# A second Strassen-Winograd level in the down projection of a two-layer block on one Trainium2 core

## Chip, core and metric

The kernel runs on one core of a Trainium2 chip. A core has five engines with an instruction queue each: TensorE (PE, the matrix multiplier; PEld is its loading of the stationary operand), VectorE (DVE), ScalarE (ACT), GpSimd (POOL) and SyncE (SP, which here issues all DMA transfers, in order). SBUF is the on-chip memory of 128 partitions, PSUM the accumulators that TensorE writes: eight banks of 128 x 512 float32 here. The metric is the device time of one execution in microseconds, as the median of several runs.

## The reference

Two blocks, A (linear attention) and B (a bilinear gated feed-forward), are applied in the order A, B, A, B with residual connections and a layer norm ahead of each. There are 2048 tokens, a width D of 1024 and a hidden width F of 3584.

```
def _B_ref(x, w_gate, w_up, w_down):
    g = x @ w_gate            # 2048x1024 @ 1024x3584
    u = x @ w_up
    return (g * u) @ w_down   # 2048x3584 @ 3584x1024

x = x + _A_ref(_layernorm(x), wqkv, wo)
x = x + _B_ref(_layernorm(x), w_gate, w_up, w_down)
x = x + _A_ref(_layernorm(x), wqkv, wo)
x = x + _B_ref(_layernorm(x), w_gate, w_up, w_down)
```

Block A projects q, k and v, applies a positive feature map to q and k, and works with sums over the tokens instead of an attention matrix. The change does not touch its arithmetic.

## The kernel before, in words

`_Prog` collects operations for each engine with the SBUF bytes and PSUM banks that they read and write, and derives the semaphore waits. Each engine's order is the order in which the code adds its operations, so the code below is a schedule written out by hand.

Block B (`layer_B`) works in two passes of 1024 tokens in each layer: four passes in all, called pass 1 to 4 here (`first` and `ps_` number them: (True, 0), (True, 1), (False, 0), (False, 1)). A pass has two stages.

`gateup` computes h = g * u. Products are taken with the Strassen-Winograd scheme, seven half-size products in place of eight: a matrix product in 2 x 2 blocks, C = A B, becomes M1 = A11 B11, M2 = A12 B21, M3 = S4 B22, M4 = A22 T4, M5 = S1 T1, M6 = S2 T2, M7 = S3 T3, where S and T are sums and differences of blocks of A and B. In passes 2 to 4 products 2 and 4 of this stage are split once more in the same way (`L2SETS`, "24"), with matmuls of 256 columns at L1044 beside those of 512 at L951. A pass has 14 pairs of weight units; the strings in `ORDERS` write out the order of each pair's steps: P, D and digits are matmul groups, F evicts a result into h and R issues two weight loads. A mark ' on a step means that it runs one pair later, so the last pair's are left over for `tail()`. The results lie in four blocks of h, hA to hD, each [128, 14, 512] in float16.

`down` multiplies h by w_down. It runs the seven products of the first level in the order 1 2 7 4 6 5 3 (`DPROD`). Each product has four blocks of 128 tokens (t = 0 to 3), and each block is 14 matmuls (two half groups of seven) into one PSUM bank: 7 x 4 x 14 = 392 matmuls of 128 x 128 by 128 x 512 in a pass, at L1199. Products alternate between the bank sets `B_DX` and `B_DV`. After a block, VectorE evicts the bank with `stt` (L624: times a scale, plus a partial sum or the residual), and makes a difference of two h blocks for a later product with `tt` (L621, 14 x 128 elements). The first product's first half group is added ahead of `tail()`.

The weights come through a ring of five SBUF slots of 8 KB a partition. `ring_issue` (DMA issues appear at L393) loads the next item into the slot that is freed next: in `gateup` a unit of gate or up weights, with its sums from DRAM; in `down` half of a product's weights (896 KB), two items a product. The w_down blocks for products 1, 2 and 3 are read from the input; the sums T for 5, 6, 7 and 4 are made once in pass 1 and kept in DRAM (`t_scratch`). The callbacks `dticks0` and `dticks1` (called for each block of a product) store x to DRAM (`stash`), run the sums that the next pass needs (`tq`, made of `t_ops` and `tp_ops`), load the weights of the next block A (`load_w`) and advance its layer norm (`nxt`).

Of the kernel before, what the change touches and what calls it, by code (L numbers as in the profile page):

```python
# [180 lines left out]
def build_kernel(nc, A_x, A_wqkv, A_wo, B_w_gate, B_w_up, B_w_down, out):  # L181
# [16 lines left out]
        "": "P1A P1B D2A F1A D2B F1B R P6A P6B T0 P7A P7B D4A F4A D4B F4B P5A F2A P5B F2B D3A F3A D3B F3B T1",  # L198
        "24": "F4A' P1A F4B' P1B 21 F3A' F3B' 25 P6A 26 T1' T0 P6B 27 D2A F1A P7A 41 P7B D2B P5A F1B P5B F2A F2B 45 46 D3A R 47 D3B D4A D4B S24+",
    }  # L200
    MUL_ENG = "pool"
    SZ_W = KT * D * 2
# [60 lines left out]
    P = _Prog(V_D + NJ * 32)  # L263
# [17 lines left out]
    KOUT = dkey("out")  # L281
    KTA = [dkey("ta%d" % i) for i in range(2)]
# [8 lines left out]
    tscr = nc.dram_tensor("t_scratch", (4, 128, NJ, 512), F16, kind="Internal").ap()  # L291
    nscr = nc.dram_tensor("xn_scratch", (S, D), F16, kind="Internal").ap()

    from contextlib import ExitStack
    with ExitStack() as es:
# [68 lines left out]
        B_DX = [7, 4, 5, 6]  # L364
        B_DV = [0, 2, 1, 3]
# [8 lines left out]
        def R(o, n):  # L374
            return [(o, o + n)]
# [204 lines left out]
        def ring_begin(first):  # L580
            RG.update(n=0, first=first, tq=None)

# [5 lines left out]
        NPASS = NU + 14  # L588
        DPROD = ["1", "2", "7", "4", "6", "5", "3"]
# [3 lines left out]

        def ring_issue():
            n = RG["n"]
            if n >= 2 * NPASS:
                return
            RG["n"] = n + 1
            o = r_slot(n)[0][0]
            ps_, u = divmod(n, NPASS)  # L600
            sl = (n + 1) % NR
            if u < NU:
# [3 lines left out]
                if not (RG["first"] and ps_ == 0):  # L606
                    dma(vh(o + 4096, 2048), sscr[u], r_slot(n, 4096, 8192), KRS[sl], rd=R(V_S + u * 32, 32))
                return
            q, hf = divmod(u - NU, 2)
            q = DPROD[q]  # L610
            js = slice(hf * 7, hf * 7 + 7)
            if q in "123":
                e, d = {"1": (0, 0), "2": (1, 0), "3": (1, 1)}[q]
                dma(vb(o, 7 * 512).rearrange("p (j c) -> p j c", c=512), wd_v[:, js, e, d * 512:(d + 1) * 512], r_slot(n, 0, 7168), KRR[sl])
            else:
                t = {"5": 0, "6": 1, "7": 2, "4": 3}[q]
                dma(vh(o, 7 * 512).rearrange("p (j c) -> p j c", c=512), tscr[t][:, js, :], r_slot(n, 0, 7168), KRR[sl],
                    rd=R(V_D + hf * 7 * 32, 7 * 32))
# [55 lines left out]
        def store_s(n):  # L674
            u = n % NPASS
# [19 lines left out]
        def layer_A(lnp, nxt, first):  # L695
# [43 lines left out]
            def lnstep(i, h):  # L739
# [638 lines left out]
```

## Time and profile before

| | us |
|---|---|
| median of three runs (1490.14 to 1492.62) | 1490.62 |
| the profiled execution's own time | 1492.19 |
| its span, first to last instruction | 1490.2 |
| PE busy | 1472.2 |
| DVE busy | 1065.6 |
| ACT busy | 479.8 |
| POOL busy | 439.0 |
| `down` of pass 1, from-to in the span | 415.4 to 500.0 |
| `down` of pass 2 | 666.7 to 752.3 |
| `down` of pass 3 | 1151.1 to 1236.7 |
| `down` of pass 4 | 1401.6 to 1487.4 |

A row of a group of instructions reads: line, engine, operation, output from input, shapes, count | busy us in all, mean ns of one | idle time of the engine just before them, and what ended it. `ps` is PSUM, `arena` is SBUF. Matmuls are pipelined: a matmul's duration in such a row is longer than the distance between the starts of two, and the distance is what a stream of them costs. A row in order of time has the start, the time to the end of the merged instructions, and in brackets the idle time before and its releaser. A row by windows has the time in the window, busy us of each engine with counts, the granted TensorE clock, the busy share of the DMA engines, and GB/s.

### The profile page before, as it was taken

The page shows a single profiled execution, that of the slowest core. Times are in us where ns is not written, and L with a number is a line of the kernel's source. Part 1 is how long each engine was busy: PE and PEld are TensorE (multiplying, and loading weights), DVE is VectorE, ACT ScalarE, POOL GpSimd, SP SyncE. Part 2 cuts the span into 40 slices and gives each one's busy share as a digit, 9 for nine tenths or more (in the row PEclk, how much of TensorE's full clock was granted, in tenths as well). Part 3 has the DMA queues.
Part 4 walks back from the last instruction along what each step waited for, and adds up shares of the span by engine and source line. Part 5 has one row for each costly group of instructions (what it writes and reads, how often), then busy time and mean ns, then how long its engine had stood idle before and what let it go on. Part 6 is the DMA issues. An engine that isn't in the chain of part 4 may idle for free.

```text
span 1490.2 us, 19805 instructions
## 1 busy us (share of the span) xinstructions
PE 1472.2 (99%) x7494; PEld 712.1 (48%) x7494; DVE 1065.6 (72%) x1862; ACT 479.8 (32%) x900; POOL 439.0 (29%) x435
## 2 busy tenths in 40 slices
PE   8999999999999999999999999999999999999999
PEld 4444444333344555554444444445555445555544
DVE  7986978778657588765488778787676565676653
ACT  3332356333300244440023314554444003444200
POOL 4544621212110144340044335314334002243300
PEclk9999999999999999999999999999999999999999
DMA  6134657698964667855465347656555655555542
GB/s 226 37 92 111 148 133 202 184 289 276 299 234 166 226 181 227 218 182 182 138 188 163 100 98 170 162 137 181 170 175 181 227 182 195 179 170 170 189 173 98
DMA packets 305263, 262.92 MB, mean 176 GB/s; under 512 B 102800, under 2 KB 266896, under 8 KB 305168
## 3 DMA queue, kind: packets, MB, share of 16 engines
q1 hardware_dynamic: 305168, 261.66, 58.4%
q8 instruction: 59, 0.97, 0.3%
q14 instruction: 36, 0.29, 0.1%
HBM read 199.23 MB, written 38.80 MB: 160 GB/s over the span
## 4 chain that ended last, share of the span: by engine, by line
PE 89%; DVE 4%; DMA 3%; issue 1%; POOL 1%; ACT 1%; SPq 0%; DVEq 0%; ACTq 0%
PE ps L951 32%; PE ps L1199 23%; PE ps L704 15%; PE ps L1044 9%; PE ps L786 7%; PE ps L872 2%; DMA arena<-arena 1%; DVE arena L621 1%; DVE arena L420 1%; DMA arena<-in_B_w_up_dram 1%; DMA arena<-in_A_wqkv_dram 1%; DMA arena<-in_B_w_gate_dram 1%; POOL arena L733 1%; PE ps L798 0%; PE ps L826 0%
## 5 line engine op out<-in xcount | busy, mean ns | idle before, releaser
L951 PE MATMUL ps<-arena 128*128 128x512 f16 x2464 | 588.6, 379 | 1.5 <-DMA arena<-in_B_w_up_dram 1.0
L624 DVE SCALAR_TENSOR_TENSOR arena<-ps,arena 128x512 f16<-128x512 f32 (+2 forms) x564 | 376.9, 687 | 239.7 <-PE ps L1199 151.2
L975 POOL TENSOR_TENSOR arena<-arena 128x512 f16<-128x512 f16 x196 | 222.9, 1164 | 453.4 <-DVE arena L624 453.3
L951 PEld LDWEIGHTS ps<-arena 128*128 128x128 f16 (+1 forms) x2464 | 232.7, 98 | 231.5 <-ACT arena L956 17.8
L1199 PE MATMUL ps<-arena 128*128 128x512 f16 (+1 forms) x1568 | 339.6, 379 | 2.4 <-DVE arena L624 2.4
L956 ACT ACTIVATE arena<-ps 128x512 f32<-128x512 f32 x308 | 183.9, 597 | 355.4 <-PE ps L951 349.9
L1199 PEld LDWEIGHTS ps<-arena 128*128 128x128 f16 x1568 | 153.2, 98 | 187.5 <-DVE arena L624 3.8
L621 DVE TENSOR_TENSOR arena<-arena 128x512 f16<-128x512 bf16 (+3 forms) x440 | 231.7, 564 | 11.4 <-DMA arena<-arena 3.6
L704 PE MATMUL ps<-arena 128*128 128x512 bf16 x1024 | 223.7, 379 | 2.8 <-ACT arena L524 1.1
L1044 PE MATMUL ps<-arena 128*128 128x256 f16 x1176 | 183.9, 273 | 3.4 <-DVE arena L621 2.2
L704 PEld LDWEIGHTS ps<-arena 128*128 128x128 f16 x1024 | 99.6, 98 | 121.7 <-DMA arena<-in_A_wqkv_dram 1.4
L1044 PEld LDWEIGHTS ps<-arena 128*128 128x128 f16 (+1 forms) x1176 | 111.0, 98 | 97.2 <-DVE ps L1051 26.7
L566 ACT ACTIVATE arena<-ps 128x512 f32<-128x512 f32 x128 | 76.4, 597 | 232.9 <-PE ps L704 218.4
L1051 DVE TENSOR_TENSOR ps<-ps,arena 128x256 f32<-128x256 f32 x168 | 72.3, 430 | 81.0 <-ACT ps L1048 76.3
L423 POOL TENSOR_SCALAR arena<-arena 128x1 f32<-128x1 f32 x64 | 20.7, 323 | 330.1 <-DVE arena L422 330.1
L786 PE MATMUL ps<-arena 128*128 128x512 bf16 x512 | 115.4, 379 | 0.0
L872 PE MATMUL ps<-arena 128*128 128x512 bf16 x512 | 111.4, 379 | 3.3 <-ACT ps L866 3.3
L733 POOL TENSOR_TENSOR arena<-arena 128x1024 f16<-128x1024 f32 x32 | 79.9, 2497 | 90.2 <-DVE arena L731 84.2
L716 POOL TENSOR_TENSOR arena<-arena 128x512 f32<-128x512 f32 x60 | 74.6, 1248 | 87.1 <-DVE arena L569 85.7
L420 DVE BATCH_NORM_STATS2 arena<-arena 128x6 f32<-128x512 bf16 x128 | 88.1, 688 | 13.1 <-DMA arena<-in_A_x_dram 6.1
L569 DVE SCALAR_TENSOR_TENSOR arena<-ps,arena 128x512 bf16<-128x512 f32 x128 | 88.5, 692 | 4.4
L567 DVE TENSOR_SCALAR arena<-arena 128x512 f32<-128x512 f32 x128 | 65.8, 514 | 27.9 <-ACT arena L566 26.6
(51 smaller groups left out, 612.9 us busy)
## 6 DMA issues: line engine op xcount, KB each, us to landing
arena<-s_scratch SPq DMA_DIRECT2D x84, 512.0 KB, 6.7
arena<-in_B_w_gate_dram SPq DMA_DIRECT2D x56, 512.0 KB, 6.1
arena<-in_B_w_up_dram SPq DMA_DIRECT2D x56, 512.0 KB, 6.2
arena<-t_scratch SPq DMA_DIRECT2D x32, 896.0 KB, 5.6
arena<-in_B_w_down_dram SPq DMA_DIRECT2D x24, 896.0 KB, 5.7
s_scratch<-arena SPq DMA_DIRECT2D x28, 512.0 KB, 6.5
arena<-in_A_wqkv_dram SPq DMA_DIRECT2D x12, 1024.0 KB, 8.1
x_scratch<-arena SPq DMA_DIRECT2D x32, 256.0 KB, 7.1
```

Source lines behind the costliest of these rows:

```text
L420: P.add("dve", (lambda h: lambda e: e.bn_stats(st[j][:, 6 * h:6 * h + 6], x_res[:, i, (D // 2) * h:(D // 2) * (h + 1)]))(h), rd=r_x(i, (D ...
L621: P.add("dve", lambda e: e.tensor_tensor(out=out, in0=a, in1=b, op=op), rd=rd, wr=wr, prd=prd)
L624: P.add("dve", lambda e: e.scalar_tensor_tensor(out=out, in0=a, scalar=sc, in1=b, op0=ALU.mult, op1=op1), rd=rd, wr=wr, prd=prd)
L704: return [e.matmul(psb(bank), xnT[:, k, i * 128:(i + 1) * 128], w[:, k, h * 512:(h + 1) * 512], start=(k == 0), stop=(k == KT - 1)) for k ...
L733: P.add("pool", lambda e: e.tensor_tensor(out=asb[b].rearrange("p (h c) -> p h c", c=32), in0=pbuf.rearrange("p (h c) -> p h c", c=32), in ...
L786: return [e.matmul(psb(bank), xr[:, t, j * 128:(j + 1) * 128], pk[:, h, t, :], start=(t == 0), stop=(t == NST - 1)) for t in range(NST)]
L872: return [e.matmul(psb(bank), xnT[:, g, i * 128:(i + 1) * 128], wp[:, g, dh * 512:(dh + 1) * 512], start=(dh == 0 and g == 0), stop=(g == ...
L951: P.add("pe", lambda e: [e.matmul(psb(bank), w[:, k, :], x[:, k, :], start=(start and k == 0), stop=(k == 3), skip_group_check=True) for k ...
L956: P.add("act", lambda e: e.activation(t, psb(bank), AF.Copy, scale=SG), prd=[bank], wr=r)
L975: P.add(MUL_ENG, lambda e: e.tensor_tensor(out=hx, in0=ut, in1=hx, op=ALU.mult), rd=ur + hr, wr=hr)
L1044: P.add("pe", lambda e: [e.matmul(psb(bank)[:, 256 * half:256 * half + 256], w[:, k, :], xx[:, k, :], start=(start and k == 0), stop=(k == ...
L1199: return [e.matmul(psb(bank), hv[:, 7 * hf + k, t * 128:(t + 1) * 128], w[:, k, :], start=(start and hf == 0 and k == 0), stop=(hf == 1 an ...
```

## The change

In passes 2, 3 and 4, products 1, 4, 5 and 3 of `down` are themselves computed by seven products of half the size in each dimension (`l2prod`). The token blocks are paired (t with t + 2, i = 0 and 1), the 14 parts of the contraction are split in two halves of seven, and the 512 output columns in two of 256. A second-level product is a sequence of seven groups, "1562734" (`DOPS`), each of 2 x 7 matmuls with 256 columns: 98 in place of 56 with 512. Groups 1, 6 and 7 accumulate in banks X, group 5 in Y, groups 2 and 3 in the two halves of A, group 4 in B. ScalarE copies X into A, B and two SBUF buffers (`acopy`), VectorE adds Y to a buffer into A and B (`dadd`), and then evicts A after group 3 and B after group 4.

The sums of h blocks (`l2sums`: four kinds for i = 0 and 1, of 7 x 128 elements each, for every second-level product) go to columns of the normalised, transposed x that the pass no longer needs. They stand in a list `bg`, together with the first level's 16 sums, and are taken from it in the numbers that the strings `POPS` give after each block or group (`pace`), or when a matmul group needs one (`need`). The first four sums of product 1 are issued in the last pair of `gateup`, at the new step H (`pre`). `POPS` also places the `tq` sums of the next pass.

The weight operands of the four products are kept ready in a new DRAM tensor, `d_images`, seven images of 7 x 256 columns each. They are made in pass 1: `make_images` takes four sums per product on VectorE out of the ring's slots, into 512-byte pieces in the same free columns, and stores them. For products 4 and 5 three raw quarters are stored from the ring as well, 22 stores in all; for 1 and 3 the raw quarters (six) are copied from DRAM to DRAM during the first block A (`raws`). In passes 2 to 4 such a product takes four ring items (two images each, the last one alone) instead of two.

The order of the products becomes 1 2 6 7 4 5 3, in pass 1 4 1 2 5 6 3 7; the bank sets become `B_DO` and `B_DS`; some PSUM accumulations and evictions move (product 7 now evicts to two destinations, and product 5 in passes 2 to 4). In pass 2 two empty ring items (`HOLES`) shift the slots. The q weights of the next block A are loaded after product 5, the k weights after group 5 of product 3, where both were loaded after product 5, k first. A second-level product calls its four ticks together at its end.

```diff
-        "24": "F4A' P1A F4B' ... D3A R 47 D3B D4A D4B S24+",
+        "24": "F4A' P1A F4B' ... D3A R 47 D3B H D4A D4B S24+",
+    DORDS = {(True, 0): "4125637", (True, 1): "1267453", (False, 0): "1267453", (False, 1): "1267453"}
+    DOPS = "1562734"
+    DL2 = {(False, 0): "", (False, 1): "1453", (True, 0): "1453", (True, 1): "1453"}
+    DIMG = "1453"
+    HOLES = {(True, 1, "6"), (True, 1, "7")}
+    PRE = "12"
+    POPS = {
+        (True, 0): "2222 2222 2222 2222 2222 2222 2222 / 0000 0000 0000 0000 1111 1111 0004",
+        (True, 1): "1111111 2222 2222 2222 2222211 2222211 2222211 /",
+        (False, 0): "1111111 2222 2222 2222 2222211 2222211 2222211 / 0 0000 1111 0000 0001111 1111111 1",
+        (False, 1): "1111111 2222 2222 2222 2222211 2222211 2222211 /",
+    }
...
-        B_DX = [7, 4, 5, 6]
-        B_DV = [0, 2, 1, 3]
+        B_DO = [4, 7, 2, 3]
+        B_DS = [0, 1, 5, 6]
...
+            elif kind == "l":
+                no = 1 if i == 3 else 2
+                qi = DIMG.index(u)
+                dma(vb(o, no * 1792), dimg[qi][:, 2 * i * 1792:(2 * i + no) * 1792], r_slot(n, 0, no * 3584), KRR[sl],
+                    rd=R(V_I + (qi * 7 + 2 * i) * 32, no * 32))
...
+                GOES = {"1": ["11"], "6": ["12"], "7": ["22", "21"] if own4 else ["22"], "4": ["21"], "2": ["11"], "5": ["22", "12"] if "3" in l2 else ["22"], "3": ["12"]}
...
+                def make_images(q, wsl):
...
+                    t1 = mk_(0, p12, p11, ALU.subtract)
+                    t3 = mk_(2, p22, p12, ALU.subtract)
+                    t2 = mk_(1, p22, st_[0], ALU.subtract)
+                    t4 = mk_(3, p21, st_[1], ALU.subtract)
+                    raws_ = [] if q in DWS else [lambda: put(*p11, "1"), lambda: put(*p22, "3"), lambda: put(*p21, "2")]
+                    return [raws_ + [t1], [t3, lambda: put(*st_[0], "5")], [t2, t4, lambda: put(*st_[2], "7")],
+                            [lambda: put(*st_[1], "6"), lambda: put(*st_[3], "4")]]
...
+                def l2prod(q, oa, sc):
...
+                    def pmm(op, i):
+                        if op in "5673":
+                            need(("s", q, "5673".index(op), i))
...
+                        bank, h, start = {"1": (X, 0, 1), "6": (X, 0, 0), "7": (X, 0, 0), "5": (Y, 0, 1), "2": (A, 0, 0), "3": (A, 1, 0), "4": (B, 0, 0)}[op]
+                        b = bank[i]
+                        (x, rx), (w, rw) = lhs(op, i), wop(op)
+                        P.add("pe", lambda e: [e.matmul(half(b, h), x[:, k, :], w[:, k, :], start=(bool(start) and k == 0), stop=(k == 6),
+                                                        skip_group_check=True) for k in range(7)], rd=rx + rw, pwr=[b])
...
+                    def after(op, i):
+                        if op == "1":
+                            acopy(half(A[i], 0), [], [A[i]], X[i])
+                        elif op in "67":
+                            c, rc = cb(2 if op == "6" else 3, i)
+                            acopy(c, rc, [], X[i])
+                            if op == "7":
+                                acopy(half(B[i], 0), [], [B[i]], X[i])
+                                dadd(i, 3, B[i])
+                        elif op == "2":
+                            dadd(i, 2, A[i])
+                        elif op == "3":
+                            fin_t(i, A[i])
+                        elif op == "4":
+                            fin_t(i + 2, B[i])
...
+                    for n, op in enumerate(DOPS):
+                        for i in range(2):
+                            pmm(op, i)
+                            after(op, i)
+                        pace(q, n)
+                        if q == "3" and op == "5" and not is_last and ps_:
+                            load_w("k", 0)
+                            load_w("k", 1)
+                        if n % 2 == 1 or n == 6:
+                            ring_issue()
...
+                    for t in range(4):
+                        ticks(q, t)
...
             def dticks0(q, t):
...
-                if q in "65":
-                    for _ in range(1 if q == "6" else 3):
-                        if tq:
-                            tq.pop(0)()
...
+                if q == o[-1]:
+                    while tq:
+                        tq.pop(0)()
...
-                    for w in "kq":
+                    for w in "q" if "3" in DL2[False, 1] else "kq":
...
+        raws = [(lambda q=q, op=op: img_raw(q, op)) for q in DIMG if q in DWS for op in "123"]
```

More of the change, by code (lines that the diff above doesn't have):

```diff
@@ L1203, in down @@
[L1203 removed]
+                            P.add("pe", fn, rd=rw + rh(ho, t, 7 * hf, 7 * hf + 7), pwr=[bank])
+                            begin()
+                            if t == 3 and hf == 0 and not img:
                                 ring_issue()
[L1205 to L1208 removed]
@@ L1244, in layer_B, with go @@
+                def go(tail):
+                    first_op[0] = tail
+                    for q in DORD:
+                        if (first, ps_, q) in HOLES:
+                            ring_issue()
+                        if q in l2:
+                            l2prod(q, B_DO, B_DS)
+                        else:
+                            plain(q, B_DS if q in "253" or (q == "4" and q in fresh) else B_DO)
+                    assert not bg
+                return pre, go
             if first:
```

351 lines of the change are left out of this document (260 added, 91 removed).

## The prediction

> **What bounds the kernel now.** I read the page first: the busy times, then the chain that ended last.
>
> ```profile
> span 1490.2 us, 19805 instructions
> ...
> PE 1472.2 (99%) x7494; PEld 712.1 (48%) x7494; DVE 1065.6 (72%) x1862; ACT 479.8 (32%) x900; POOL 439.0 (29%) x435
> ...
> PE ps L951 32%; PE ps L1199 23%; PE ps L704 15%; PE ps L1044 9%; PE ps L786 7%; PE ps L872 2%; DMA arena<-arena 1%; DVE arena L621 1%; DVE arena L420 1%; DMA arena<-in_B_w_up_dram 1%; DMA arena<-in_A_wqkv_dram 1%; DMA arena<-in_B_w_gate_dram 1%; POOL arena L733 1%; PE ps L798 0%; PE ps L826 0%
> ```
>
> TensorE is busy for 99% of the span, and 23% of the chain is L1199, the w_down matmuls. So an instruction taken from TensorE there is time, unless a wait takes its place. The three passes that matter, all engines (columns: time, then PE, PEld, DVE, ACT, POOL busy, granted clock, DMA share, GB/s):
>
> ```profile
> 415.40:500.00 84.60, 84.60 (x393) 38.35 (x392) 47.52 (x65) 0.00 (x0) 2.78 (x3) 1.00 0.57 195
> 666.70:752.30 85.60, 84.81 (x394) 38.32 (x393) 47.42 (x65) 0.00 (x0) 6.11 (x9) 1.00 0.53 180
> 1401.70:1487.50 85.80, 84.88 (x393) 38.10 (x391) 42.47 (x56) 0.00 (x0) 4.53 (x4) 1.00 0.44 153
> ```
>
> A pass is TensorE and nothing else: VectorE rests 37 us of 85, ScalarE does nothing, the DMA engines are half used. These three rests are what the change spends. Groups by line with shapes kept apart give the prices:
>
> ```profile
> L1199 PE MATMUL ps<-arena 128*128 128x512 f16 x896 | 194.0, 379 | 0.0
> L1044 PE MATMUL ps<-arena 128*128 128x256 f16 x1176 | 183.9, 273 | 3.4 <-DVE arena L621 2.2 <-DVE ps L1051 1.2
> L1199 PE MATMUL ps<-arena 128*128 128x512 bf16 x672 | 146.9, 379 | 2.4 <-DVE arena L624 2.4
> L1051 DVE TENSOR_TENSOR ps<-ps,arena 128x256 f32<-128x256 f32 x168 | 72.3, 430 | 81.0 <-ACT ps L1048 76.3 <-PE ps L1044 2.6
> L621 DVE TENSOR_TENSOR arena<-arena 128x1792 f16<-128x1792 f16 x64 | 69.2, 1082 | 3.1 <-POOL arena L975 3.1
> L1048 ACT COPY ps<-ps 128x256 f32<-128x256 f32 x168 | 62.4, 371 | 49.9 <-PE ps L1044 43.1 <-DVE arena L624 4.4 <-PE ps L951 2.4
> L1044 PEld LDWEIGHTS ps<-arena 128*128 128x128 f16 x672 | 62.0, 97 | 53.0 <-DVE ps L1051 24.0 <-ACT ps L1048 6.4 <-DVE arena L621 2.0
> L624 DVE SCALAR_TENSOR_TENSOR arena<-ps,arena 128x512 f32<-128x512 f32 x80 | 53.8, 689 | 59.9 <-PE ps L1199 59.4
> L621 DVE TENSOR_TENSOR arena<-arena 128x512 f16<-128x512 f16 x94 | 43.6, 473 | 1.2
> L621 DVE TENSOR_TENSOR arena<-arena 128x2048 f16<-128x2048 f16 x16 | 19.5, 1216 | 3.6 <-DMA arena<-arena 3.6
> ```
>
> **1. The matmuls, -16.8 us.** 896 + 672 = 1568 matmuls are four passes of 392, seven products of 56. A pass without a gap takes 84.60 us, so a matmul costs 84.60/392 = 0.216 and a product 12.09. A second-level product issues 7 x 2 x 7 = 98 matmuls half as wide. The instruction durations (379, 273) are pipelined; the price is the distance between starts, which the gate/up stage, where such matmuls run now, shows in order of time:
>
> ```profile
> 501.73 0.60 PE L1044 MATMUL ps<-arena 128*128 128x256 f16 x4
> 502.17 1.03 PE L951 MATMUL ps<-arena 128*128 128x512 f16 x4
> ...
> 504.12 0.82 PE L1044 MATMUL ps<-arena 128*128 128x256 f16 x6
> 504.77 0.59 PE L951 MATMUL ps<-arena 128*128 128x512 f16 x2
> ```
>
> Four take 0.44 and six 0.65, so 0.109 each, and a product 98 x 0.109 = 10.68. Saved: 1.40 on each of 4 x 3 products.
>
> The Trainium skill (TensorE: Matmul & The Clock Gate, section Back-to-back issue gap) says that in a stream of weight loads and matmuls both set the spacing, with 81 ns at 128 columns and 131 ns at 512. Interpolated, an estimate of 98 ns at 256, three quarters of a wide one; a product would then cost 0.75 x 98/56 = 1.31 of today's, and this term be +45 us instead of a gain. The trace does not agree, with 0.216 and 0.109, an even half.
>
> **2. Inside a second-level product, 0.** ScalarE gains 8 copies of 0.37 per product, in a stage where it shows 0.00. VectorE gains four additions (L1051, 0.43) and eight sums of 7 x 128 elements. No row has that size; it lies between 0.47 (512 elements) and 1.08 (1792), and on the line through both at 0.66. Product 5, the dearest, then has 8 x 0.66 (the sums for product 3) + 4 x 0.43 + 8 x 0.69 (two evictions a block) = 12.5 against TensorE's 10.7. The excess of 1.8 is passed on to product 3, which has no sums to make (4 x 0.43 + 4 x 0.69 = 4.5). TensorE waits only where an addition must precede matmul group 3, or where a bank must be evicted. Groups (two blocks of seven matmuls) end every 1.53: group 2 is the fourth, ended at 6.1, and group 3 starts at 7.6; the sums tied to group 6 (ended 4.6) are done by 5.8 and the two additions by 6.6, 1 us in time. In the third pass twelve more sums (the T operands of the next pass) stand among these, four (0.47 or less) in product 4, four in 5. VectorE then leaves product 4 about 4.2 late, at 14.8; four sums and three or four T sums (3.6) bring it to the first addition at 18.4, done at 18.8, where group 3 is due at 10.6 + 7.6 = 18.2. **+0.65**, between 0 and, with sums of 1.08, about 5.
>
> **3. The start of a second-level pass, -1.8.** Today each start has a hole (TensorE first, VectorE below):
>
> ```profile
> 667.82 0.59 PE L1199 MATMUL ps<-arena 128*128 128x512 bf16 x2
> 669.20 1.04 PE L1199 MATMUL ps<-arena 128*128 128x512 bf16 x4 [0.79 <-DVE arena L624]
> ```
>
> ```profile
> 665.81 0.43 DVE L1051 TENSOR_TENSOR ps<-ps,arena 128x256 f32<-128x256 f32 x1 [0.88 <-ACT ps L1048]
> 666.72 0.69 DVE L624 SCALAR_TENSOR_TENSOR arena<-ps,arena 128x512 f16<-128x512 f32 x1 [0.48 <-PE ps L1044]
> 668.45 0.69 DVE L624 SCALAR_TENSOR_TENSOR arena<-ps,arena 128x512 f16<-128x512 f32 x1 [1.04 <-PE ps L1199]
> ```
>
> The product begins on bank 7, which the last gate/up eviction still reads: 0.79, in passes 2 to 4. After the change group 1 begins on banks 0 and 1, free by then, so the hole goes. New is that four sums stand on VectorE ahead of the late evictions (they need the last POOL product of hA, long done): 666.24 + 4 x 0.62 = 668.7, first late eviction ended 669.4, ScalarE's copy into its bank 669.8, and group 6, which overwrites the copy's source, is due at 666.74 + 4 x 0.763 = 669.8. So 0.2 each is left: 3 x (0.2 - 0.79). With sums of 1.08 it is 1.9 each, so this term lies between -2.4 and +3.3.
>
> **4. Pass 1 to pass 2, +1.5.** The twelve sums are now taken late: the last four, for operand "2", run after product 7's last block, which also has two evictions instead of one.
>
> ```profile
> 500.21 0.69 DVE L624 SCALAR_TENSOR_TENSOR arena<-ps,arena 128x512 bf16<-128x512 f32 x1 [2.33 <-PE ps L1199]
> 500.82 1.55 DVE L621 TENSOR_TENSOR arena<-arena 128x512 f16<-128x512 bf16 x4
> ```
>
> Today the weight sums of the first pair start 0.81 after TensorE's last w_down matmul (500.01). Then: 0.2 + two evictions (1.25) + four sums of 0.39 (1.55) = 3.0 and 0.4 for the first weight sum, 3.4. Step "25" needs it after P1A, P1B and "21", 1.95. Between 0 and 2.5.
>
> **5. Layer B to layer A, +2.35.** In pass 2 the block-wise ticks of product 3 (layer norm of four tiles) now run together at its end, because a second-level product calls them after all its groups.
>
> ```profile
> 750.10 0.54 DVE L440 TENSOR_SCALAR arena<-arena 128x1024 f16<-128x1024 bf16 x1
> 750.55 1.41 DVE L420 BATCH_NORM_STATS2 arena<-arena 128x6 f32<-128x512 bf16 x2
> 752.00 0.21 DVE L422 BATCH_NORM_AGGREGATE arena<-arena 128x2 f32<-128x12 f32 x1
> 752.51 0.69 DVE L624 SCALAR_TENSOR_TENSOR arena<-ps,arena 128x512 bf16<-128x512 f32 x1 [0.30 <-PE ps L1199]
> ...
> 755.15 0.37 DVE L567 TENSOR_SCALAR arena<-arena 128x512 f32<-128x512 f32 x1
> 755.55 0.69 DVE L569 SCALAR_TENSOR_TENSOR arena<-ps,arena 128x512 bf16<-128x512 f32 x1
> ```
>
> Four times 1.6 (statistics) and twice 0.45 (normalise) are 7.3 after the last eviction (0.75 past the end T of TensorE's work): 8.05, then 1.1 for the first projection's evacuation: T + 9.2. The projections turn over four banks of 8 matmuls, so the fifth is due at T + 6.9: 2.35. Today the burst ends at T + 2.8. The k weights come later too: q first, k only after group 5 of product 3, T - 7.5. With 3.1 us per MB the halves land near T + 0.6 and T + 3.6, which delays the first four projections but, since the fifth waits for VectorE anyway, adds nothing. If the DMA is 3 us later, 3 more. Between 0 and 6.
>
> **6. Transfers.** The rows for what DMA can carry:
>
> ```profile
> arena<-t_scratch SPq DMA_DIRECT2D x32, 896.0 KB, 5.6
> arena<-in_B_w_down_dram SPq DMA_DIRECT2D x24, 896.0 KB, 5.7
> ...
> arena<-in_A_wqkv_dram SPq DMA_DIRECT2D x12, 1024.0 KB, 8.1
> ```
>
> ```profile
> 140.00:150.00 10.00, 10.00 (x57) 4.88 (x55) 9.45 (x12) 1.37 (x3) 8.29 (x3) 1.00 0.61 120
> 300.00:310.00 10.00, 10.00 (x48) 4.10 (x47) 6.64 (x14) 3.07 (x7) 0.00 (x0) 1.00 1.06 335
> 740.00:750.00 10.00, 10.00 (x48) 4.57 (x47) 5.59 (x10) 0.00 (x0) 1.58 (x4) 1.00 1.07 341
> ```
>
> A second-level product reads seven images of 459 KB in 10.7 us, 301 GB/s, twice today's rate, against some 320 at a full share (335/1.06). Each load is issued when its slot is free, 10.7 us before its use, and lands in 5.7: hidden. Only SP's order bites: output stores wait for late evictions of product 5 in pass 3, with the next pass's first gate loads behind them: **+0.3**, between 0 and 3.
>
> In pass 1 come 22 stores of 459 KB in runs of 512 bytes, a price no row has. The window at 300, mostly 512-byte loads, gives 1.45 us each; the one at 140, transposes, 197 GB/s and 2.33. I take the first, which has the same run length. Today's share is 0.57 x 84.6 = 48.2; with 22 x 1.45 = 32 it is 80 of 84.6. Product 4's seven stores make a queue of some 5 us, against a lead of 13.6 us for the ring's loads: 0. The 16 image sums (17.3 us of VectorE, waiting for stage buffers still being stored) fit beside 47.5 of 84.6; an eviction delayed by up to 9 us costs nothing, since products alternate between two sets of banks. The six copies from DRAM to DRAM go out in the first projections, where the DMA has room: 0.
>
> **Sum.** -16.8 - 1.8 + 0.65 + 1.5 + 2.35 + 0.3 = -13.8. The profiled execution took 1492.19 (span 1490.2), so 1478.4 for one like it; the median of the runs shown is 1490.62, 1.6 lower, so 1476.8.
>
> **Rivals.**
> (a) The waits of 3 to 5 do not come because VectorE's queue overlaps better than counted: -16.8 - 2.4 = -19.2, 1471.4. For it: back-to-back sums run 0.08 faster than their means (1.55 for four). Chance 0.09.
> (b) VectorE sets the pace in products 4 and 5, sums nearer 1.08: then product 5 needs 15.9 against 10.7. Say half of that excess, 2.6, in three passes: -13.8 + 7.8, 1484.6. For it: h is read in pieces of 128 elements, and 0.66 is interpolated. Against it: 1082 and 1216 ns for 1792 and 2048 such elements are nearly all slope. Chance 0.17.
> (c) Loads of images fall behind: were only two in flight, 5.7/2 a load, the rate still holds; one in flight, 4 x 5.7 = 22.8 a product. A loss of 1 us per product gives 1488.8. Chance 0.05.
> (d) On the other side: the stores of pass 1 saturate the DMA. At 2.33 they need 51.3 + 48.2 = 99.5, 15 more than the pass, and loads behind them add a landing of 5.7: 1476.8 + 20.6 = 1497.4. A store of 1.65 fills the pass (22 x 1.65 + 48.2 = 84.6), and from 2.28 the gain is gone. For it: nothing here stores runs of 512 bytes. Chance 0.07.
> (e) Half-wide matmuls pay their weight load: 0.097 + 0.109 = 0.206, a product 20.2, +97 us, 1588. The rows of L1044 speak against it: 0.109 with the loads running. Chance 0.02.
> The Trainium skill (TensorE: Matmul & The Clock Gate, section Back-to-back issue gap), quoted above, points towards (e), with 98/56 x 98/131 in place of its price.
>
> The forecast itself has 0.60.
>
> The measurement can tell about 0.2% (3 us) from no change. Faster by more: (a), the forecast, (b) and half of (c), 0.88. Same: 0.03. Slower: (d) and (e), 0.09. The range for 8 in 10 reaches from (a), 1471, to past (b), 1486.
>
> **What would show it.** PE at about 1455 us busy with 1568 - 12 x 56 = 896 wide and 1176 half-wide matmuls on w_down; passes 2 to 4 near 79 us; sums of 896 elements near 0.62 on VectorE; no 0.79 hole at the starts, but about 1.5 after pass 1 and 2.4 in the first projections of the second layer A; DMA share near 0.95 in pass 1. It is wrong if TensorE shows idle time inside products 4, 5 or 3, or waits for ring loads in pass 1.

## The result, and the profile after

| | before | after |
|---|---|---|
| median of six runs of each on one chip | 1491.41 (1490.14 to 1492.62) | 1481.93 (1479.86 to 1483.31) |
| ratio, 95% interval | | 0.9934 [0.9922, 0.9947] |
| the profiled execution's own time | 1492.19 | 1482.65 |

The change gains 9.5 us (0.66%), two thirds of the 13.8 us forecast. The page of the changed kernel:

```profile
span 1480.9 us, 21214 instructions
...
PE 1459.8 (99%) x7998; PEld 761.8 (51%) x7998; DVE 1150.7 (78%) x2018; ACT 513.0 (35%) x996; POOL 443.1 (30%) x435
...
L1460 PE MATMUL ps<-arena 128*128 128x256 f16 (+1 forms) x1176 | 130.2, 273 | 1.9 <-DVE ps L1470 1.9
...
L1392 PE MATMUL ps<-arena 128*128 128x512 f16 (+1 forms) x896 | 194.0, 379 | 0.0
```

TensorE is 12.4 us less busy (1472.2 before). The four `down` stages, a window each (time, then PE, PEld, DVE, ACT, POOL busy, granted clock, DMA share, GB/s):

```profile
414.20:498.80 84.60, 84.60 (x394) 38.36 (x393) 59.12 (x72) 0.00 (x0) 3.60 (x3) 1.00 0.98 314
667.00:748.00 81.00, 79.43 (x562) 54.47 (x559) 67.24 (x104) 11.01 (x32) 5.25 (x4) 1.00 0.75 252
1151.20:1231.10 79.90, 79.26 (x562) 54.59 (x560) 72.43 (x115) 11.02 (x32) 5.25 (x4) 1.00 0.76 259
1397.90:1477.60 79.70, 79.06 (x560) 54.39 (x559) 66.02 (x103) 11.01 (x32) 5.25 (x4) 1.00 0.65 230
```

The span falls into stages at the first matmul of each (A block A, g `gateup`, d `down`; numbers count the passes, layer 1 has A1 to d2; each includes the wait at its end):

| | A1 | g1 | d1 | g2 | d2 | A2 | g3 | d3 | g4 | d4 |
|---|---|---|---|---|---|---|---|---|---|---|
| before | 241.46 | 172.57 | 84.61 | 166.73 | 85.57 | 231.32 | 167.48 | 85.57 | 164.97 | 88.59 |
| after | 241.51 | 171.30 | 84.61 | 168.17 | 81.10 | 232.02 | 171.11 | 79.96 | 166.79 | 82.98 |

d2 to d4 give 15.7 us; g2, A2, g3 and g4 take 7.6 back. The holes that do it are few. Ahead of group 3 of a pass's first second-level product (TensorE, VectorE and POOL in order of time; pass 2 here, passes 3 and 4 alike):

```profile
666.95 7.81 PE L1460 MATMUL ps<-arena 128*128 128x256 bf16 x70
675.40 3.32 PE L1460 MATMUL ps<-arena 128*128 128x256 bf16 x28 [0.64 <-DVE ps L1470]
```

```profile
666.36 2.22 DVE L670 TENSOR_TENSOR arena<-arena 128x896 f16<-128x896 f16 x4
668.50 2.65 DVE L673 SCALAR_TENSOR_TENSOR arena<-ps,arena 128x512 f16<-128x512 f32 x4
671.06 3.94 DVE L670 TENSOR_TENSOR arena<-arena 128x896 f16<-128x896 f16 x3
674.92 0.75 DVE L1470 TENSOR_TENSOR ps<-ps,arena 128x256 f32<-128x256 f32 x2
```

```profile
669.26 5.25 POOL L1026 TENSOR_TENSOR arena<-arena 128x512 f16<-128x512 f16 x4 [2.82 <-DVE arena L673]
```

The same 896-element sum takes 0.55 when four run alone (2.22) and 1.31 when three run beside POOL's products (3.94; singly 0.95, 1.57 and 1.57), so the two additions that group 3 waits for come late. After pass 1 (first two rows), from layer B to layer A (next two) and from pass 3 to pass 4 (last):

```profile
501.45 0.39 PE L1095 MATMUL ps<-arena 128*128 128x256 f16 x2 [0.79 <-DVE arena L670]
502.12 0.39 PE L1095 MATMUL ps<-arena 128*128 128x256 f16 x2 [0.28 <-DVE arena L670]
...
748.05 1.90 PE L753 MATMUL ps<-arena 128*128 128x512 bf16 x8 [0.97 <-DMA arena<-in_A_wqkv_dram]
750.81 2.55 PE L753 MATMUL ps<-arena 128*128 128x512 bf16 x11 [0.87 <-DMA arena<-in_A_wqkv_dram]
...
1233.81 1.04 PE L1002 MATMUL ps<-arena 128*128 128x512 f16 x4 [1.65 <-DMA arena<-in_B_w_gate_dram]
```

The largest loss lies where nothing was changed, between the second block A and pass 3. Before, then after, with the window that follows:

```profile
985.93 0.39 PE L1044 MATMUL ps<-arena 128*128 128x256 f16 x2 [0.42 <-DVE arena L621]
988.07 0.39 PE L1044 MATMUL ps<-arena 128*128 128x256 f16 x2 [1.74 <-DVE arena L621]
...
991.76 0.38 PE L1044 MATMUL ps<-arena 128*128 128x256 f16 x2
```

```profile
983.22 0.39 PE L1095 MATMUL ps<-arena 128*128 128x256 f16 x2 [1.26 <-DVE arena L670]
985.35 0.60 PE L1095 MATMUL ps<-arena 128*128 128x256 f16 x2 [1.75 <-DVE arena L670]
...
991.84 0.38 PE L1095 MATMUL ps<-arena 128*128 128x256 f16 x2
```

```profile
985.00:990.00 5.00, 4.65 (x14) 2.04 (x15) 3.23 (x8) 1.13 (x3) 0.00 (x0) 0.50 0.00 0
```

The layer norm chain at the end of block A did not move forward as far as TensorE did, so the first hole grew by 0.84. Then the granted clock was 0.50, from 984.2 to 991.1: from the end of the second hole to the same matmul in the sequence it takes 6.49 (985.35 to 991.84) in place of 3.69 (988.07 to 991.76), 2.8 more.

### The profile page after: what moved, and what is told of

Its sections match the earlier page's. It is cut to its first block, busy times and chain, and to the rows that moved or that the text cites. A ratio compares the mean times of both kernels' runs of the same rounds, so it can differ in the third digit from the quotient of the medians.

```text
span 1480.9 us, 21214 instructions
## 1 busy us (share of the span) xinstructions
PE 1459.8 (99%) x7998; PEld 761.8 (51%) x7998; DVE 1150.7 (78%) x2018; ACT 513.0 (35%) x996; POOL 443.1 (30%) x435
## 4 chain that ended last, share of the span: by engine, by line
PE 86%; DVE 6%; DMA 4%; issue 1%; POOL 1%; SPq 1%; ACT 1%; DVEq 0%; ACTq 0%
PE ps L1002 33%; PE ps L753 15%; PE ps L1392 13%; PE ps L1095 9%; PE ps L837 7%; PE ps L1460 6%; PE ps L923 2%; DVE arena L670 2%; DMA arena<-arena 1%; DVE arena L435 1%; DMA arena<-in_B_w_gate_dram 1%; DVE arena L673 1%; DMA arena<-in_A_wqkv_dram 1%; POOL arena L782 1%; SPq L408 1%
## 5 line engine op out<-in xcount | busy, mean ns | idle before, releaser
L673 DVE SCALAR_TENSOR_TENSOR arena<-ps,arena 128x512 f16<-128x512 f32 (+2 forms) x560 | 371.0, 687 | 126.5 <-PE ps L1002 53.4
L1026 POOL TENSOR_TENSOR arena<-arena 128x512 f16<-128x512 f16 x196 | 225.9, 1180 | 449.6 <-DVE arena L673 449.5
L670 DVE TENSOR_TENSOR arena<-arena 128x512 f16<-128x512 bf16 (+5 forms) x552 | 309.8, 604 | 16.0 <-DMA arena<-arena 4.3
L1392 PE MATMUL ps<-arena 128*128 128x512 f16 (+1 forms) x896 | 194.0, 379 | 0.0
L753 PEld LDWEIGHTS ps<-arena 128*128 128x128 f16 x1024 | 99.9, 98 | 124.1 <-DMA arena<-in_A_wqkv_dram 3.1
L1392 PEld LDWEIGHTS ps<-arena 128*128 128x128 f16 x896 | 87.7, 98 | 105.1
L1460 PE MATMUL ps<-arena 128*128 128x256 f16 (+1 forms) x1176 | 130.2, 273 | 1.9 <-DVE ps L1470 1.9
L1460 PEld LDWEIGHTS ps<-arena 128*128 128x128 f16 x1176 | 114.6, 98 | 17.2 <-DVE ps L1470 2.8
```

Of the source, the lines that this page charges most:

```text
L670: P.add("dve", lambda e: e.tensor_tensor(out=out, in0=a, in1=b, op=op), rd=rd, wr=wr, prd=prd)
L673: P.add("dve", lambda e: e.scalar_tensor_tensor(out=out, in0=a, scalar=sc, in1=b, op0=ALU.mult, op1=op1), rd=rd, wr=wr, prd=prd)
L753: return [e.matmul(psb(bank), xnT[:, k, i * 128:(i + 1) * 128], w[:, k, h * 512:(h + 1) * 512], start=(k == 0), stop=(k == KT - 1)) for k ...
L1026: P.add(MUL_ENG, lambda e: e.tensor_tensor(out=hx, in0=ut, in1=hx, op=ALU.mult), rd=ur + hr, wr=hr)
L1392: return [e.matmul(psb(bank), hv[:, 7 * hf + k, t * 128:(t + 1) * 128], w[:, k, :], start=(q in fresh and hf == 0 and k == 0), stop=(hf == ...
L1460: P.add("pe", lambda e: [e.matmul(half(b, h), x[:, k, :], w[:, k, :], start=(bool(start) and k == 0), stop=(k == 6), skip_group_check=True ...
```

## The experiments

Every kernel is the changed kernel with one or more edits, timed beside the kernel before. The changed kernel itself spreads over 5 us: its eleven runs here go from 1479.86 to 1485.0 with a median of 1482.44. A difference of one or two us is therefore read from holes and stages in the trace, not from medians.

**Control.** The changed kernel again, with no edit.

> The changed kernel once more, unaltered, as the control for the runs beside it. Theory (the sum of the prediction with its terms corrected from the profile: matmuls -16.4, three holes of about 0.7, pass 1 to 2 +1.4, layer B to A +1.8, pass 3 to 4 +1.8, second layer A to B about +3): 9 to 10 us below the kernel before. If the step from the second layer's block A to its block B (3.6 us longer in the profile, and the TensorE clock at half for 3.4 us) is chance, this profile shows it under 1.5 us longer and the clock at full; if the change causes it, it is there again.

1483.43 (1481.27 to 1485.0), ratio 0.9947 [0.9934, 0.9959]. The junction shows holes of 1.22 and 1.74 and a granted clock of 0.66 in the window that had 0.50; g3 is 169.71. The loss recurs, so it is not one bad execution; its size varies with how long the clock stays down (3.4 us here, 6.8 in the profile after).

**1. The hole ahead of group 3.**

```diff
-P.add(MUL_ENG, lambda e: ... hx = ut * hx)
+P.add("dve" if l2 and p == NU // 2 - 1 and dst in "43" else MUL_ENG, ...)
```

> Passes 2 to 4: the four late products of the last pair (h = u * h, 128 x 512) run on VectorE instead of GpSimd. Theory 1, VectorE's 16-bit sums and GpSimd's products take turns at SBUF: the sums of product 1 that took 0.95, 1.57 and 1.57 take 0.62 again, the hole of 0.64 ahead of group 3 goes although VectorE has four more operations of 0.4 to do, and the time falls by about 1.5 to 2 us against the control. Theory 2, VectorE is simply late because it has too much to do there: the four more operations make the hole larger, by about 1.6 in each of three passes, and the time rises by 3 to 5 us.

1479.59 (1479.34 to 1480.2), ratio 0.9923 [0.991, 0.9937]. TensorE and VectorE in pass 2:

```profile
673.55 4.75 PE L1460 MATMUL ps<-arena 128*128 128x256 f16 x42 [0.24 <-issue]
```

```profile
672.49 0.43 DVE L1026 TENSOR_TENSOR arena<-arena 128x512 f16<-128x512 f16 x1
672.83 1.69 DVE L670 TENSOR_TENSOR arena<-arena 128x896 f16<-128x896 f16 x3
674.43 0.76 DVE L1470 TENSOR_TENSOR ps<-ps,arena 128x256 f32<-128x256 f32 x2
```

VectorE now also does POOL's four products (0.43 each) and is still done earlier: three sums take 1.69 in place of 3.94. The two engines had been taking turns; more work on one of them is faster than sharing. The hole ahead of group 3 is gone; one of 0.24 stands ahead of group 7, where the profile names no releaser. By the holes that is worth 0.4 a pass. In this profile the first hole of the junction is gone too, for another reason: the clock fell ahead of it, after one wait of 2.00 at the end of block A, and while TensorE ran slowly the layer norm caught up (the order of events in the trace; no run tests it).

```profile
960.00:965.00 5.00, 5.00 (x18) 1.99 (x17) 2.68 (x7) 4.94 (x7) 0.79 (x2) 0.73 0.40 78
```

**2. From layer B to layer A: two waits, or one over the other?** First the k weights ahead of the q weights (which no longer go out after product 5), then the ticks of product 3 called after its groups 2, 7, 3 and 4 and not together at its end, then both.

```diff
 if q == "3" and op == "5" and not is_last and ps_:
     load_w("k", 0)
     load_w("k", 1)
+    load_w("q", 0)
+    load_w("q", 1)
...
+if q == "3" and n >= 3:
+    ticks(q, n - 3)
```

> Pass 2: the q weights of the next block A are loaded after the k weights instead of before; both start after group 5 of product 3. Theory 1 (two waits lie over each other: the k weights land late, and behind them VectorE's burst of layer norm holds the fifth projection): the waits of 0.97 and 0.87 on the weights go, but a wait of about 2.0 to 2.4 for a bank takes their place at the fifth projection, and the time is the same within 0.6 us of the changed kernel. Theory 2 (the weights alone are late): the time falls by 1.8 us.

> Pass 2: the four ticks of product 3 (layer norm of four tiles, stash of x) are called after its groups 2, 7, 3 and 4 instead of all after the last. Theory 1: VectorE's burst is gone from the start of block A (first projection evacuated near T + 5 instead of T + 8.5), but TensorE still waits 0.97 and 0.87 for the k weights, and the time is the same within 0.6 us. Theory 2 (the burst alone costs): the time falls by 1.8 us.

> Both edits together. Theory 1: only now both waits are gone, the time falls by about 1.8 us against the changed kernel, and the start of the second block A has no hole over 0.3. If either edit alone already gave the 1.8, theory 1 falls.

k first 1481.13 (1479.45 to 1483.14), ticks spread 1483.36 (1480.79 to 1484.95), both 1479.83 (1479.14 to 1481.52). The waits of TensorE, with k first, with the ticks spread, and with both:

```profile
755.73 9.45 PE L753 MATMUL ps<-arena 128*128 128x512 bf16 x43 [1.97 <-DVE arena L584]
```

```profile
748.04 1.90 PE L753 MATMUL ps<-arena 128*128 128x512 bf16 x8 [1.16 <-DMA arena<-in_A_wqkv_dram]
750.87 14.42 PE L753 MATMUL ps<-arena 128*128 128x512 bf16 x66 [0.93 <-DMA arena<-in_A_wqkv_dram]
```

```profile
754.41 10.96 PE L753 MATMUL ps<-arena 128*128 128x512 bf16 x50 [0.19 <-DVE arena L584]
```

The two waits lie over each other. Taking one away uncovers the other at nearly its size (1.97 against 0.97 + 0.87); only both edits free the place. Even then d2 and A2 together take 312.93, against 313.12 in the profile after and 314.01 in the control. In this profile too the clock fell at the end of block A, behind a wait of 1.95 for ScalarE, which hides the gain. In experiment 8, with both edits and no such fall, they take 311.35, 1.8 less than in the profile after; 0.4 of that is experiment 1's.

```profile
955.00:960.00 5.00, 4.03 (x12) 1.50 (x13) 2.60 (x6) 3.34 (x6) 0.79 (x2) 0.67 0.67 183
```

**3. After pass 1.** The last four sums of operands are dealt out between the weight sums of the first pair, not all ahead of them.

```diff
-... 1111 1111 0004
+... 1111 1111 0000
...
-c["sums24"]()
+c["sums24"](late_t)      # a weight sum and an operand sum in turn
```

> Pass 1 to pass 2: the last four T sums are not run ahead of the four weight sums of the first pair, but one by one between them, in the order in which TensorE's steps need them. Theory (prediction, part 4): the hole of 0.95 + 0.44 at the first pair's steps comes from the order of eight sums behind two evictions; interleaved, the first step's operands are ready 1.1 us earlier, the hole shrinks to 0.2 to 0.5, and the time falls by 0.9 to 1.2 us. Rival: the weight sums wait for the gate loads (DMA share 0.98 in pass 1); then the hole stays.

1483.61 (1481.59 to 1484.18), ratio 0.9947 [0.9935, 0.9959]; g2 168.58 in place of 168.15 in the control.

```profile
503.08 0.61 PE L1100 MATMUL ps<-arena 128*128 128x256 f16 x4 [1.66 <-DVE arena L670]
```

The expectation fell. Two steps wait there, one after the other. In the profile after, "21" starts behind the third operand sum (the hole of 0.79), and "25" behind the first weight sum, which comes two sums later (0.28). Dealt out, the third operand sum is the sixth of the eight and not the third, so "21" starts 3.55 after pass 2's first matmul (499.53 to 503.08) in place of 2.67 (498.78 to 501.45). By the code, "21" multiplies only a quarter of the operand that these sums do not change (`b11`), but declares all of it as read (`rx`), and the third sum writes another quarter. So this wait may come from the declared range and not from the data; no run narrows the range.

**4. From pass 3 to pass 4, and after pass 1 again.** First the operand sums of pass 3 taken earlier, so that VectorE has fewer ahead of its last evictions:

```diff
-... / 0 0000 1111 0000 0001111 1111111 1
+... / 0 0000 1111 1111 0000000 0000000 1111
```

> Pass 3: the eight T sums that stood in products 4 and 5 stand in products 7 and 3. Theory 1, VectorE lateness in product 5 holds back the output stores, and SP's order holds the next pass's first gate loads behind them: the loads are issued 3 to 4 us earlier, the wait of 1.65 on them at the start of pass 4's gate/up stage goes, time falls by 1.5 to 1.9 us against the control. Theory 2, the loads are late because the DMA engines are full (image loads at 301 GB/s): the wait stays, no difference.

1481.42 (1480.04 to 1485.17). The hole stays (first rows), because the gate weights are still issued (SP's queue, next rows) behind stores of the output:

```profile
1229.16 1.03 PE L1002 MATMUL ps<-arena 128*128 128x512 f16 x4
1232.01 1.04 PE L1002 MATMUL ps<-arena 128*128 128x512 f16 x4 [1.83 <-DMA arena<-in_B_w_gate_dram]
```

```profile
1221.33 1.53 SPq L408 DMA_DIRECT2D out_dram<-arena  x2
1222.90 0.46 SPq L408 DMA_DIRECT2D arena<-in_B_w_gate_dram  x1
1223.40 1.56 SPq L408 DMA_DIRECT2D arena<-s_scratch  x1
1225.01 0.43 SPq L408 DMA_DIRECT2D arena<-in_B_w_gate_dram  x1
```

The stores go out 7.8 ahead of pass 4's first matmul (1221.33 to 1229.16), exactly as in the profile after, so VectorE's extra sums were not what held them. So SP's order was taken itself, and with it, at the other place, the last four operand sums of pass 1, one product earlier:

```diff
-dma(out2[i * 128:(i + 1) * 128, c:c + 512], xs, [], KOUT, rd=rx)
+OUTQ.append([0, put_out])    # pass 3: issued after the second ring load that follows
...
-... / 0000 0000 0000 0000 1111 1111 0004
+... / 0000 0000 0000 1111 1111 1111 0000
```

> Two edits at two places. In the third pass the output stores go on SP's queue behind the next one or two loads, not ahead of them. In the first pass the last four sums of operands for pass 2 are taken one product earlier, not after the last block. Pass 3 to 4: if SP's order holds the gate weights back (the second load is issued 0.5 to 1.4 us late), the wait of 1.0 to 1.65 falls to under 0.5; if the slot or the load on the DMA engines sets it, it stays. Pass 1 to 2: if the first step of pass 2 waits for the third of those operand sums and then for a weight sum, as the run with the sums interleaved suggests, both holes (0.95 and 0.44) go and the stage of 168.15 becomes 166.7; if the weight sums alone set it, 0.4 or more stays. Together 1480 to 1481 against 1482 to 1483.

1479.42 (1477.55 to 1480.08), ratio 0.9917 [0.9902, 0.9932]. The early sums lie in the same 8 KB as partial results that product 7's eviction still needs, and write over part of them; so this changes what is computed, but not the work, and tells a time and no version for use. TensorE at both places, and SP:

```profile
498.61 1.89 PE L1011 MATMUL ps<-arena 128*128 128x512 f16 x8
500.33 0.60 PE L1104 MATMUL ps<-arena 128*128 128x256 f16 x4
...
1230.07 1.89 PE L1011 MATMUL ps<-arena 128*128 128x512 f16 x8
1231.80 0.60 PE L1104 MATMUL ps<-arena 128*128 128x256 f16 x4
```

```profile
1219.56 0.38 SPq L408 DMA_DIRECT2D arena<-in_B_w_gate_dram  x1
...
1222.62 0.39 SPq L408 DMA_DIRECT2D arena<-in_B_w_gate_dram  x1
```

Both holes are gone, and g2 (166.75) and g4 (164.97) are what they were before the change. Reckoned back from pass 4's first matmul, the first gate load goes out 10.5 ahead in place of 6.3 (with the edit of VectorE's sums alone, and in the profile after); in the profile before it was 24.0 (1212.69 to 1236.67).

**5. The junction and the clock.** Six and eight matmuls that nobody reads are put into the two holes.

```diff
+if not first and ps_ == 0 and p == 0 and tk in ("P1B", "21"):
+    pairs[0]["fill"](6 if tk == "P1B" else 8)
```

> At the start of the second layer's block B, 6 and 8 matmuls of 512 columns, whose result nobody uses, stand ahead of the two steps of the first pair that wait for VectorE (1.3 and 1.7 us of work in holes of 1.26 and 1.75). Theory 1, TensorE's clock falls to half because of these two holes: with fillers the granted clock stays at full there, the eight following matmuls start 0.216 apart instead of 0.43, and the time falls by about 1.7 us in executions that had the drop (0 to 1.7 in the median). Theory 2, the clock drop has another cause, or is chance: it remains or comes and goes without the fillers too; the time is the same or up to 1 us longer because the fillers overrun the holes.

1480.66 (1479.41 to 1484.01), ratio 0.9933 [0.992, 0.9947]. The window behind the holes:

```profile
985.00:990.00 5.00, 4.98 (x30) 2.59 (x28) 4.46 (x12) 1.84 (x4) 0.00 (x0) 1.00 0.09 18
```

The clock stays at 1.00 and g3 is 168.26 (171.11 and 169.71 without the filling). All profiles together: eight of the changed kernel and its variants have both holes of the junction unfilled, and the clock falls at them in six (after, control, ticks spread, sums interleaved, stores behind loads, and experiment 7) and not in two (sums of pass 3 moved, k first). In experiment 7's profile the first hole is only 0.58:

```profile
1000.25 0.39 PE L1098 MATMUL ps<-arena 128*128 128x256 f16 x2 [0.58 <-DVE arena L673]
1002.38 0.39 PE L1098 MATMUL ps<-arena 128*128 128x256 f16 x2 [1.74 <-DVE arena L673]
```

There the granted clock is 0.50 from 1003.3 to 1006.7. In the two profiles where the first hole is 0.4 (before, and experiment 6) it does not fall, nor in the two where the first hole had closed and one of 1.43 or 1.74 was left (experiment 1, and both edits of 2). In the two with filling, this one and that of 8, it does not fall either; but two of eight kept it without filling, so two are few. The holes allow the drop and do not force it.

**6. The matmuls alone.** All products of passes 2 to 4 at one level again; order, banks, images and stores remain. The empty ring items go, and `POPS` of these passes is written for blocks again.

```diff
-DL2 = {(False, 0): "", (False, 1): "1453", (True, 0): "1453", (True, 1): "1453"}
+DL2 = {(False, 0): "", (False, 1): "", (True, 0): "", (True, 1): ""}
```

> Passes 2 to 4 of the changed kernel with all seven products at one level (56 wide matmuls each); product order, PSUM banks, weight images (still made and stored, no longer read) and the sums of pass 1 stay. Theory 1 (the gain is the matmuls', and the losses come with the second-level products): each of the twelve products costs 1.37 more, +16.4; the three holes ahead of group 3 (0.64 each), the two waits on the k weights (1.84) and most of the wait on the gate weights (1.65) go; the holes after pass 1 (1.4) stay. That is 1482.6 + 16.4 - 1.9 - 1.8 - 1.5 = about 1494, with TensorE busy for 1472, as in the kernel before. Rival (order and banks carry part of the gain): under 1489.

1492.96 (1491.05 to 1494.2, ten runs), ratio to the kernel before 1.0012 [1.0002, 1.0022]. The start of pass 2:

```profile
668.65 83.27 PE L1392 MATMUL ps<-arena 128*128 128x512 bf16 x381 [0.79 <-DVE arena L673]
```

The old hole of 0.79 is back, d2 and d3 are 85.35, A2 230.98, g3 167.69 and g4 165.18, near those of before; g2 keeps its loss (168.38). So the redrawn order and the images gain nothing by themselves: the medians put their cost at some 2 us, and the profile, which is of the fastest of the ten runs, shows 1.65 of it after pass 1. What is gained in d2 to d4 comes with the second level's matmuls, and the losses in A2, g3 and g4 too. Only g1 is shorter here as well (171.01 against 172.57).

**7. The stores of pass 1.** Each store of an image is issued twice, the second time into a tensor that nothing reads.

```diff
 P.add("sp", lambda e: e.dma_start(dst, ...), ...)
+P.add("sp", lambda e: e.dma_start(dst2, ...), ...)
```

> Every store of an image in pass 1 is issued twice, the second time into a tensor that nobody reads: 22 more stores of 459 KB in runs of 512 bytes. Theory 1 (a store costs the DMA engines 1.45 us and the share of 0.98 in pass 1 is a full one): 32 us more on 83 in a pass of 84.6; at the largest share that the trace shows (1.07) that needs 107, so the pass grows by some 15 to 23, less what drains into the stage behind it. Rival (the share overstates the load and there is room): the pass grows by under 3.

1500.08 (1498.45 to 1501.71), ratio 1.0058 [1.0037, 1.0078]. Pass 1 by its window, and TensorE's waits in it:

```profile
414.20:516.20 102.00, 88.38 (x389) 38.78 (x392) 59.27 (x72) 0.00 (x0) 3.09 (x3) 0.95 1.06 332
```

```profile
440.92 10.75 PE L1395 MATMUL ps<-arena 128*128 128x512 bf16 x48 [1.41 <-DMA arena<-in_B_w_down_dram]
...
457.51 26.03 PE L1395 MATMUL ps<-arena 128*128 128x512 f16 x111 [2.59 <-DMA arena<-t_scratch]
491.33 24.50 PE L1395 MATMUL ps<-arena 128*128 128x512 bf16 x104 [7.79 <-DMA arena<-in_B_w_down_dram]
```

The pass grows from 84.6 to 102.0: 13.6 of it TensorE waits, and 3.8 are matmuls slowed behind these waits (granted clock 0.95 on average). So the share of 0.98 was nearly a full one (here it is 1.06), and the change stands just at the edge of what the DMA engines carry there.

**8. The edits together:** those of 1, 2, 4 (stores and early sums, which write over partial results here too) and 5.

> The edits that took a wait away, together: late products of each second-level pass on VectorE, k weights first and the layer norm's steps spread over product 3, unused matmuls in the holes at the second junction from layer A to layer B, output stores behind the loads, the four sums early. If the gains add up: 0.4 x 3 for the late products, up to 1.5 at the layer change (part of it given back at the end of block A, as the run with both edits showed), 1.4 after the first junction, about 1 at pass 3 to 4 and 0 to 2 for the clock: 1476 to 1478. If they only move the wait to the next late thing: 1479 to 1480, the level of the best single edits.

1473.43 (1472.5 to 1473.81), ratio 0.9878 [0.9863, 0.9893]. Pass 1 to 2 and pass 3 to 4 are closed, d2 is 79.66, g3 167.99. The gains add up, past what was expected. This too tells a time and no version for use. With the four early sums left where the change has them, 1.4 would come back (the step in g2 above): an estimate of 1474.8 for a kernel that would beat both and was not run. To take them early they would need 3 KB elsewhere.

## Why the prediction was right, point by point

The time fell inside the range; it lies 5.1 above the point. The profiled execution is 9.5 shorter, and the terms as measured add up to that: -16.4 -0.45 +1.44 +1.84 +1.8 +3.6, and -1.3 in g1, where waits for gate and up weights went from 1.5 to 0.4 (one profile of the kernel before; all thirteen profiles of the changed kernel and its variants have 170.57 to 171.31 in g1, but no run shows which part of the change would do it).

1. **The matmuls, -16.8: right.** A hole shown as 0.79 cost 0.96 before (85.57 against 84.61), so the one of 0.64 costs 0.81, and d3 without it is 79.15: 5.46 a pass, 1.37 a product, 16.4 in all. Experiment 6, without them, is no faster than the kernel before. Rival (e) fell by the same rows. The figures of the Trainium skill (TensorE: Matmul & The Clock Gate, section Back-to-back issue gap) pointed towards it; this trace does not agree, with 16.4 less and not 45 more.
2. **Inside a product, +0.65: 0.** The sum of 896 elements takes 0.55 on average in a run of four (2.22), in place of 0.66, and no hole stands at product 5. VectorE as the bound, rival (b), fell.
3. **The starts, -1.8: -0.45.** The old hole went as said, but 0.64 stands at group 3. The step that failed is that the sums keep their time: 0.62 was no less than it takes alone, and the price beside POOL's late products, 1.31 on average, lay in no row that I had used. Experiment 1 shows it, with 3.94 against 1.69 for three sums. The Trainium skill (SBUF — State Buffer, section Who interferes with whom) says that a VectorE instruction with two SBUF inputs contends with a GpSimd instruction that reads SBUF; the trace agrees, by the same two numbers. The bound of +3.3 held it.
4. **Pass 1 to 2, +1.5: +1.44.** Right, and the place as well: "25" starts 3.34 after pass 2's first matmul (498.78 to 502.12), where I had reckoned 3.4. That "21" ahead of it waits too, for an operand sum, I had not seen, and experiment 3 failed on it.
5. **Layer B to A, +2.35: 1.84,** but it is the k weights that TensorE waits for, where I had let VectorE set the fifth projection. Experiment 2 shows that both were there, one over the other: 1.97 for VectorE once the k weights come early.
6. **Transfers, +0.3: 1.8** (g4 164.97 to 166.79). The step was right (gate loads behind output stores on SP's queue), its size six times too small, inside its bound of 3. For pass 1, rival (d) fell: 22 stores cost no time. Experiment 7 shows how near it was: 22 more cost 17.4. The window from which I took the 1.45 was not mostly 512-byte loads: they are 2048 of its 3460 packets, but 31% of its bytes.
7. **What no term had: +3.6 at the second junction.** I had moved all later stages forward with TensorE and taken no stage for one whose other chains stay behind. 0.84 of it is such a hole, and 2.8 the clock that fell behind it.

The forecast was low because terms 3 and 6 were taken near their cheap end (2.9 together), term 1 came out 0.4 smaller, and one place was left out (3.6). That the range still held is in part luck: terms 2, 4 and 5 came out 1.2 cheaper than forecast, and g1, where no term stood, 1.3 shorter.

## What to carry to other kernels

When a stage is made shorter, list what else ends with it: each chain that ran level with TensorE (layer norm, weight loads behind stores) becomes a hole of its own. Here g2, A2, g3 and g4 took back 7.6 of 15.7 us, 2.8 of it through the clock. Price an instruction by what runs on its neighbour at that time, not by its mean; moving POOL's products onto VectorE made VectorE finish earlier. Where two waits lie over each other, test both edits together, since either alone gains next to nothing.

## What the runs showed of the hardware that was not expected

- VectorE's sums and POOL's products, both from SBUF to SBUF in 16 bits, take turns: three sums in 3.94 beside POOL, 1.69 without.
- The granted clock fell to 0.50 at holes of 1.26 and 1.75 with 0.4 of work between them, once at 0.58 and 1.74, and in two other profiles behind single waits of 2.00 and 1.95. It stayed at 1.00 in two of the eight profiles with both holes, and behind a single wait of 1.97 (k first). It stayed down for 3.4 us, in the profile after for 6.8. The Trainium skill (TensorE: Matmul & The Clock Gate, section What's actually happening) names a free-running window of about 3.4 us as the idle time needed. The traces do not agree on the length: a wait of 2.0, or two that end within 3.4 us of the first one's start (981.96 to 985.35), were enough in some executions.
- Stores of 512-byte runs: 22 more in pass 1 raised the DMA engines' work from 0.98 x 84.6 = 82.9 to 1.06 x 102 = 108.1, 25 us, so at least 1.15 a store, against 1.45 estimated. At least, because the window moved only 7.3 MB more (332 x 102 against 314 x 84.6) where the 22 stores are 10.1 MB, so some transfers slid out of it. A packet of 512 bytes in that window lasts 27.8 ns on average; by that a store, 896 of them on 16 engines, is an estimated 1.55.
